# K loads of 512 KB for each batch step in place of 1 MB for two, with the order table written anew

## The chip, the cores and the metric

The kernel runs on one core of one Trainium2 chip. The metric is the device time of one execution in microseconds; the number compared is the median over runs. The profile shows one execution: its span is the time from the first to the last instruction that the profiler saw.

Names of the engines in the profile: PE is TensorE (matmuls; PEld its weight loads), DVE VectorE, ACT ScalarE, POOL GpSimd, SP the queue of SyncE, from which this kernel starts all of its DMAs. L645 is line 645 of the kernel.

## What is computed

Two independent problems A and B of the same shape, each an attention block over a given key and value cache, with their outputs side by side:

```python
B, Sq, D = 16, 80, 576
Hq, Hkv, Sk, Dh = 32, 16, 512, 128
q = (x @ wq).reshape(B, Sq, Hq, Dh).transpose(0, 2, 1, 3)
k = repeat(k_cache, 2, axis=1); v = repeat(v_cache, 2, axis=1)
p = softmax(einsum("bhqd,bhkd->bhqk", q, k) * Dh ** -0.5)
o = einsum("bhqk,bhkd->bhqd", p, v)
out = o.transpose(0, 2, 1, 3).reshape(B, Sq, Hq * Dh) @ wo      # concatenated: (16, 80, 1152)
```

All arrays are bf16. A K or V cache is 16 x 16 heads of 512 x 128, that is 128 KB a head and 32 MB a problem.

## The kernel before

**Steps.** The work is cut into 128 steps U (64 a problem). A step is one batch element and four key heads (eight query heads). Steps alternate between two groups of four heads: U = 2i and U = 2i + 1 are the same batch element with heads 4q to 4q+3 and 4q+4 to 4q+7 (line 500). Eight batch elements make a half of the batch.

**A step.** The Q projection for four batch elements and one pair of heads at a time (L565 and its tail L578 on PE, evicted to `qT` by L590 on ACT or L591 on DVE). The scores of a step are five tiles of 128 x 512: one of the remainder rows (L679, the 4 x 32 rows that don't fit in the four main tiles; one PE operation does it for two steps together) and four main tiles (L692), one for each key head. Each tile gets its row maximum on DVE (L701), the exponential with row sums on ACT (L705), a reciprocal on DVE (L711) and the scaling on POOL (L714). For two steps together the tiles are transposed on PE (L749), copied to `pT` (L766, L767, L775, L776), multiplied with V (L797), and copied to `oT` (L811, on ACT or DVE). Then comes the output projection (L843), gathered in `acc` (L855) and at the end added and stored (L872, L878).

**Loads.** All DMAs are issued by SP, in one order. K is loaded by a transposing DMA (L645) into `kT`, which holds NK = 6 steps in three pairs of slots; V by plain DMAs of 512 KB (L649) into six slots. With KSP = 0 the width `kw` (L637) is 2 for every step: the even step of a pair issues one transfer of 1 MB that writes the slots of both steps, with one semaphore, and the odd step issues none (L651). Besides these there are loads of wq (L534), its tail (L538), wo (L608) and x (L400; for problem B L461, L466, L467), and the stores.

**The order.** Every operation belongs to a stream (for example all K loads, or all exponentials). `ORDER` (L61) is a string that merges the streams into one order: each letter takes the next operation of its stream, an apostrophe ahead of it puts that operation on ACT in place of DVE where it may run on either, and digits are PSUM banks. Every engine and SP run their operations in this order. Letters that matter here: `a` K load, `m` V load, `Q` wo, `R`, `S`, `T` wq, `U`, `V`, `W` wq's tail, `X` x, `O` store; `e`, `f`, `d` Q projection for the first, the second and the later groups of heads (`h`, `i`, `g` its tails), `j` main scores, `k` remainder scores of a pair, `l` transposes, `c` product with V, `b` output projection.

The dependencies and semaphores follow from the order (`finalize`, L214). Two rules bear on loads: a load waits for the last readers of the slots that it writes (for K the scores of six steps before), and `paced` operations, that is all whose name starts with `ld`, wait for the PE operation that stands last ahead of them in the order (L240):

```python
if op.eng == "pe":
    last_pe = op
elif op.paced and last_pe is not None:
    deps[id(last_pe)] = last_pe
```

Of the kernel before, what the change touches and what calls it, by code (L numbers as in the profile page):

```python
# [66 lines left out]
cc7cc4cmmammj6d0j2wKAwd7'Bt'Btgl4315NwKCtl6G'F'Hk27F'E'Gj3j4xNwwb6j1ubtwtxj2aj3c0cNw'ytw'Atj6mc4Qcc5Qcj0d1j2tw
ANBwDCCCDCCc3mcCutd5BCtgl3674'HwNKFl0DCj5t'F'Ej1j2b3bGwNwGwtCCt'ytj5d7c0wNj6j3cwttwc4d2cs1j5CDCc6AYNwct'BCCc1'
ActCgml0436'H'K'Gl5Fk27'B'F'EGk40xj1b5wuxtxNxuuCCabc2j6mj3uwwNyd7j4cd1gwtt'Ac5j6HNwt'Ktcj0j3b2wj4wBNbc7j1twtCC
CDCDCycj5tCNwl6320'Atl4wF'Gj7c1tcmwEd3j6d5'Ft'Ggj7c2BNwNwaj0'Htj1j4cmwtc3AKNwwtDCCCCCCDCcd6c2cad7c0'BttAcCgl25  # L70
13K'B'Hl4F'Gk06'EFj2'Gj7xc4mb1j5cmbj3wuxNwt'Auj4Nwwwtt'yCCj0j2ac6cc7cj5md1tBNAwwtwNtCCDCCCDj7b6twd4c3bcttCg'yl
7520BH'Kl6G'Fk31'Ek47'F'Gxxc2mj5uxuNNwDCCCCcb6j0ubtAwxj2c1'ytwcc3j4cc5'Buj0tNwAwCDCcd1j6md2d3ttwNBd4tCggCl6057
'K'H'Kal2NHGE'G'F'Fk31j4b0Cxwuj2c6cmc7j5twxctuAwj4j3btwBNwd1j6Uj2aj7b5Ctwttc4Rj3wNwDCCt'ytcbj2d6AwtwNCDCCCc7cd
4mt'B'yd0ggl2537NKH'Hmml6j4NGEwb1CDCCCj3bj5w'F'K'GtFwtc7cj6c3j2c'y'AtNwwBtj7c4j0d5cmUc6tcj3wwNwBd1d2'AttCCCDCd
7tggl4360H'K'HKl5F'Gak17'Ek23'F'Gxc4xucc6cUj0b5j1u'AxNwBxwututCDc7cj2AwNRmbj4c0j7cj3j1b6twNwt'y'BtwNCCCCCCCDwd
2bj4d5tywttd6amd3ggl7041'K'KNHHl2'Gk63E'Fj0'F'Gxxj5uc7cuNwwAj2c4j1cc6mc'Bc3tcj4b7Ut'Bwtd5j3wNwAtd0wCCDCCCCj2tw
NDCtj6bd4wtd1tNyCggl6723'HNKK'Hl0'G'FDCCCk15'F'GEaj4j7xuxwc2cj0c6mcj3b1wAwu'Btttc6cmj5mj4bwNwAwtd7j0twNtj6d2DC
CCCCwc5d3ctd4atggyBNH'K'Hl6501CCDKNl7'Gj3Ew'Fj2j5j4c6'G'Fcc0cj1c7ct'AwBwwtj0c6c'Att'BwNb2d3j7d5j4CtCCCwNwwCtab
d6DCt'ytd7ggml2401H'K'KHl3F'Gk67'Ek24x'F'Guxc5j0cb3wxNu'Atuc6cbj7c0cmCCBxwyNuj1c6mmcj5wt'B'Atj3d2Nwwtb4j7j1d6d
5j0btwwwNCDCCDCCCttNytd7aQggl0143NK'HCCCKl2F'G'Hk76Ej0'F'Gj1xCDc5xucc4cj3j2c7Aww'Butwtwb5maj4bcj1twNwAtj0d3j6c  # L80
2Qmcd7CDCtwwNtCCtd1ByNtd4gDCCHgl6520'H'KNKFl3'Gk41'Ej5'G'Fxj7mCuxwwc2cc0cj3j6'Auttac4cb2BAwwd0j5j1j4mbc7twNtwt
tNwj3d6cCCCCDwtd1Cd5tBygKNgl2437'H'H'Gl6FNE'K'G'Fj0b1CCwj2j3twwj5Qbj6mc0twcd2c7cj4'yttwNAwCCDCt'Btd3j1c5gcj6Nw
wd0c4md7cCCDC'AttKHgl3526mmBH'Kl1F'Gk04Gk73'F'Exab1j5c2cc6xuxuwNDCCcj4j0bNBxwwu'Atuc6cj2j7c5tAwNwDCCCCtj3acb4t
'Bd6j0twNwd5mj2btd3tzwNztd0gOgl2471'H'HCCCCKKl6'Fk03Exx'Gj5j2c4'G'FcuAwNwuc7j6cj1QOc0mc'Bc3tcj7b4Aw'BttwwNj0j5
ad2btwtwNj6td3CCDDCCCwzNtd1COd7tggl6540'K'Hl3'FKHNGk12'ECCCj5'Gxj6mXj7'Fj4xc0ucwc3ucc1ctb2j5wAww'BtttAwNj3bXd1
j0j6CwtzwNwttd4c7mcd3aOtd2DCDCCBNgCgl6705KK'Hl1NHE'G'FCCd2j4j7wwj0c6cc3c'F'GBwt'Atj1c5j4cXj3c6cwNww'At'Bttb7j6
# [870 lines left out]
```

## Time and profile before

| | |
|---|---|
| median of 3 runs | 716.97 us (712.87 to 717.15) |
| the profiled execution, its own time | 715.38 us |
| its span | 712.3 us |
| PE, ACT, DVE, POOL busy | 703.7, 647.0, 614.7, 432.6 us |
| granted TensorE clock | 1.00 throughout |
| K loads: issues, median from issue to landing | 32 of A, 8.9 us; 32 of B, 8.5 us |
| V loads: issues, median from issue to landing | 64 of A, 5.2 us; 64 of B, 5.4 us |

How to read it: a row of a group has the line, engine and operation, the tile written and those read, the shapes, the count, the busy time, the mean of one in ns, and the idle time ahead of them with what ended it. A row of a tile or line has the least, median and largest duration of one in ns, and the first and last start. A row of the timeline or of the chain starts with the start and the length in us. A row of waits has the total, the count and the longest. A row of windows has the stretch, its length, the busy time of PE, PEld, DVE, ACT and POOL, the granted clock, DMA's share and GB/s. A matmul's duration includes its way through the array, so neighbours overlap; the pace of a sequence is read from a chain piece divided by its count.

### The profile page before, as it was taken

How to read it: one execution, taken by the hardware profiler on the slowest of the kernel's cores; microseconds unless marked ns; L12 is line 12 of the kernel's file. 1: busy time of each engine (PE TensorE's matmuls, PEld its weight loads, DVE VectorE, ACT ScalarE, POOL GpSimd, SP SyncE). 2: the span in 40 equal slices, each digit the busy share in tenths (PEclk: the TensorE clock that was granted, in tenths of full speed). 3: DMA queues.
4: the chain of work that ended last, by engine and by line, in shares of the span. 5: the costliest groups of instructions: out<-in, count | busy, mean ns of one | idle time of the engine just before them, and what ended most of it. 6: DMA issues, size and time to landing. Idle time of an engine off the chain costs nothing.

```text
span 712.3 us, 26078 instructions
## 1 busy us (share of the span) xinstructions
PE 703.7 (99%) x10820; PEld 511.9 (72%) x10820; DVE 614.7 (86%) x1337; ACT 647.0 (91%) x1774; POOL 432.6 (61%) x650
## 2 busy tenths in 40 slices
PE   8999999999999999999999999999999999999998
PEld 4567767777776777777767777777777777777777
DVE  2999988888898988889989889898889989899894
ACT  2999989899998999989999899999999999999893
POOL 0667666657565575556766566665755666566663
DMA  9999999998999999999979999999999968898872
GB/s 216 261 249 262 256 230 249 285 220 212 205 229 263 240 227 226 197 261 243 240 204 210 278 247 226 198 194 260 254 209 268 219 161 234 211 254 162 225 166 73
DMA packets 374165, 160.70 MB, mean 226 GB/s; under 512 B 278560, under 2 KB 370976, under 8 KB 374048
## 3 DMA queue, kind: packets, MB, share of 16 engines
q1 hardware_dynamic: 374048, 159.05, 96.5%
q8 instruction: 85, 1.39, 0.8%
q14 instruction: 32, 0.26, 0.1%
HBM read 87.65 MB, written 2.95 MB: 127 GB/s over the span
## 4 chain that ended last, share of the span: by engine, by line
PE 92%; ACT 5%; DMA 2%; DVE 1%; issue 0%
PE ps L843 21%; PE ps L797 19%; PE ps L565 18%; PE ps L692 15%; PE ps L749 10%; PE ps L679 4%; ACT p_sb L705 4%; PE ps L578 3%; DMA kT<-in_B_k_cache_dram 2%; ACT pT L766 1%; ACT qT L590 1%; PE ps L373 1%; PE ps L421 0%; ACT pT L775 0%; ACT oT L811 0%
## 5 line engine op out<-in xcount | busy, mean ns | idle before, releaser
L714 POOL TENSOR_SCALAR p_sb<-p_sb,rinv 128x512 bf16<-128x512 bf16 x640 | 430.8, 696 | 264.0 <-DVE rinv L711 263.6
L705 ACT ACTIVATE p_sb<-ps,negmax 128x512 bf16<-128x512 f32 x640 | 440.1, 720 | 14.6 <-DVE negmax L701 12.1
L701 DVE TENSOR_REDUCE negmax<-ps 128x1 f32<-128x512 f32 x640 | 411.3, 680 | 20.7 <-PE ps L692 12.9
L797 PE MATMUL ps<-pT,v_sb 128*128 128x160 bf16 x2048 | 184.7, 233 | 0.5 <-issue 0.4
L797 PEld LDWEIGHTS ps<-pT,v_sb 128*128 128x128 bf16 x2048 | 154.4, 98 | 39.1 <-ACT pT L775 2.9
L843 PE MATMUL ps<-wo_sb,oT 128*128 128x288 bf16 x1280 | 180.1, 286 | 0.3 <-ACT pT L766 0.3
L692 PE MATMUL ps<-kT,qT 128*128 128x512 bf16 x512 | 169.0, 380 | 1.7 <-ACT p_sb L705 0.9
L565 PE MATMUL ps<-xT,wq_sb 128*128 128x320 bf16 x1024 | 167.5, 299 | 0.7 <-DVE xT L429 0.5
L843 PEld LDWEIGHTS ps<-wo_sb,oT 128*128 128x128 bf16 x1280 | 122.9, 98 | 42.9 <-ACT pT L766 2.2
L705 ACT ACTIVATION_READ_ACCUMULATOR p_sb<-ps,negmax 128x1 f32 x640 | 150.5, 235 | 0.0
L565 PEld LDWEIGHTS ps<-xT,wq_sb 128*128 128x128 bf16 x1024 | 96.8, 98 | 43.5 <-ACT p_sb L705 2.0
L766 ACT COPY pT<-ps 128x512 f32<-128x512 f32 x182 | 99.6, 602 | 6.3 <-PE ps L749 4.4
L749 PEld LDWEIGHTS ps<-ident,p_sb 64*128 64x128 bf16 x5120 | 82.7, 95 | 8.0 <-issue 1.3
L591 DVE TENSOR_SCALAR qT<-ps 128x320 bf16<-128x320 f32 x125 | 56.9, 484 | 36.3 <-PE ps L578 35.9
L749 PE MATMUL ps<-ident,p_sb 64*128 64x64 bf16 x5120 | 86.0, 190 | 0.5 <-DVE qT L591 0.5
L590 ACT ACTIVATE qT<-ps 128x320 bf16<-128x320 f32 x131 | 52.7, 443 | 24.2 <-PE ps L578 23.9
L811 DVE CAST oT<-ps 128x320 bf16<-128x320 f32 x135 | 64.3, 481 | 9.0 <-PE ps L797 8.8
L692 PEld LDWEIGHTS ps<-kT,qT 128*128 128x128 bf16 x512 | 45.2, 97 | 30.6 <-ACT pT L766 5.4
L811 ACT CAST oT<-ps 128x320 bf16<-128x320 f32 x121 | 53.3, 453 | 1.9 <-PE ps L797 1.7
L767 DVE COPY pT<-ps 128x1024 bf16<-128x1024 bf16 x74 | 49.3, 685 | 4.8 <-PE ps L749 4.3
L711 DVE RECIPROCAL rinv<-rowsum 128x3 f32<-128x3 f32 (+1 forms) x256 | 40.2, 161 | 4.0 <-ACT p_sb L705 3.6
L679 PE MATMUL ps<-kT,qT 128*32 128x512 bf16 x512 | 37.0, 383 | 1.0 <-DMA kT<-in_B_k_cache_dram 1.0
(33 smaller groups left out, 151.4 us busy)
## 6 DMA issues: line engine op xcount, KB each, us to landing
v_sb<-in_A_v_cache_dram SPq DMA_DIRECT2D x64, 512.0 KB, 5.2
v_sb<-in_B_v_cache_dram SPq DMA_DIRECT2D x64, 512.0 KB, 5.4
wo_sb<-in_A_wo_dram SPq DMA_DIRECT2D x8, 576.0 KB, 5.7
wo_sb<-in_B_wo_dram SPq DMA_DIRECT2D x8, 576.0 KB, 5.0
wq_sb<-in_B_wq_dram SPq DMA_DIRECT2D x4, 1024.0 KB, 6.9
out_dram<-osb SPq DMA_DIRECT2D x40, 72.0 KB, 3.7
wq_sb<-in_A_wq_dram SPq DMA_DIRECT2D x8, 256.0 KB, 4.4
wq_sb<-in_A_wq_dram SPq DMA_DIRECT2D x2, 1024.0 KB, 6.9
```

The costliest lines, as they stand in the source:

```text
L565: last = e.matmul(ps[:, vbq[h].phys, QO:QO + 320], lhsT=wq_sb[:, wsl, ck, hi * 128:(hi + 1) * 128], rhs=xT[:, half, ck, n0:n0 + 320], star ...
L590: return e.activation(dst, src, AF.Identity, scale=SCALE)
L679: last = e.matmul(ps[32 * g4:32 * g4 + 32, vb_.phys, :], lhsT=qT[:, qsl_, bl_, g4 * 160 + 128:g4 * 160 + 160], rhs=k_of(U_, g4), start=Tru ...
L692: return e.matmul(ps[:, vb.phys, :], lhsT=qT[:, qsl, bl, gl * 160:gl * 160 + 128], rhs=k_of(U, gl), start=True, stop=True)
L701: return e.tensor_reduce(negmax[:, si:si + 1], ps[:, vb.phys, :], axis=AX.X, op=AluOpType.max, negate=True)
L705: return e.activation(p_sb[:, psl, :], ps[:, vb.phys, :], AF.Exp, bias=negmax[:, si:si + 1], scale=1.0, accum_out=rowsum[:, ss, k:k + 1])
L714: return e.tensor_scalar(p_sb[:, psl, :], p_sb[:, psl, :], rinv[:, ss, k:k + 1], 1.0, op0=AluOpType.mult, op1=AluOpType.mult)
L749: last = e.matmul(dst, lhsT=p_sb[64 * h:64 * h + 64, psl2[i_][k_], j * 128:(j + 1) * 128], rhs=ident[64 * h:64 * h + 64, 64 * h:64 * h + 6 ...
L766: return e.copy(dst.bitcast(F32), ps[:, vb.phys, :].rearrange("p (j n) -> p j n", j=4))
L797: last = e.matmul(ps[:, vo.phys, off:off + 160], lhsT=v_sb[:, vs, gl, j * 128:(j + 1) * 128], rhs=pT[:, pts, j, :, 32 * gl:32 * gl + 32], ...
L811: return (e.copy if en == "act" else e.tensor_copy)(dst, src)
L843: last = e.matmul(ps[:, vb.phys, 0:DC], lhsT=oT[:, sp_ * (HH // 2) + i, rb * 128:(rb + 1) * 128], rhs=wo_sb[:, 2 * c3 + sp_, i, :], start= ...
```

## The change

Two lines of code change, two constants and the order table. `kw` is now 1 for steps with KSA <= U // 2 < KSP, which is all of them, so each of the 128 steps issues its own transposing DMA of 512 KB into its own slot, with its own semaphore; the place of the data in `kT` is as before. The wait for a slot's last readers and the pacing now hold for each step by itself. Nothing else in the code changes.

```diff
-KSP = 0
+KSA = 0
+KSP = 64
...
-            kw = 2 if goct >= ILV and U // 2 >= KSP else 1
+            kw = 1 if KSA <= U // 2 < KSP else 2
...
-                      dsem="d_k%d" % ks, name="ldk%d" % U, stream="K")
+                      dsem="d_k%d" % ks, name="ld%s%d" % ("hk"[kw - 1], U), stream="K")
```

The functions around it, unchanged:

```python
def em_ldk(e, kc_ap=kc_ap, b=b, q=q, ks=ks, w=kw, il=goct >= ILV):
    src = kc_ap[b, 4 * q:4 * q + 4 * w, :, :].rearrange("g (p j) d -> (g p) j d", j=4)
    if il:
        dst = kT[:, ks // 2, :].rearrange("p (j n) -> p j n", j=4)[:, :, ks % 2 * 512:(ks % 2 + w) * 512]
    ...
    return e.dma_start_transpose(dst, src)
```

The order table is replaced as a whole: 5180 operations before, 5244 after, the 64 added ones all K loads. Its first three lines, before and after:

```diff
-XXSSVVTvv!PSSan2o7o3PZo5'ZZTe6o2e4r5o7!ZZYe0e3WWhIThf1'J'IJe4e6Te0he7e2r5hae3'I'I'J'YJe4e7hhf0'I'I'Jmj5j6k2wxJ
-tf4f3uiwij7'M'Ltj5wLf2f1j0X'MtNwtif4wMLj7f6tiaCCwNj5'MXf1m'LwCDCtk3j0xf6twiuLj4'Mtj2NwDCCj5e7j3e0wwNtthwk46'Jt
-Ixl1027tCC!xul5Gj3'Ff4maGNwp1'Fu'EDj7Zwf5ij1j2mc0ctLwNt'Atc6j3cj4e7wNwBte0hj6twNIw'J'MtCCCDCCCCC!aj2j1c3cc0cw'
...
+XSSVVSSXTvv!Pn3r1o4o7o5'ZYPZ'Ze2e6aTTWWTe1e3e7he5e4hI'JI'Je0hf2ho3o6'J'Z'JIIZf5aaaaXaj6wj4j1j0mk7f3wtwtmf6f4tw
+xuf1i'Mtiie7NLLNL'Me2f5!CDCf0'Mj1iwr3'Mj4'LYk0f6j5wtxtwuj3Xamhf1j4Iw'Jte0j7wwtj2e5tmhaij3twINk70me4NMwCCCCDCCx
+t'J'Lte1hj3j6uxINwNwl7425'Juj1'Gf0Fwtf4til7Ltk63FxNCCDCCCCj0ae7j1'G'Ewutc2cwj6f5At'Me0f2p4wNxCCDtihaj1c6u'L'IZ
...
```

More of the change, by code (lines that the diff above doesn't have):

```diff
@@ L67 @@
[L67 to L86, printed above, removed]
@@ new lines @@
+ZtCcxc6cC'Axl0247uBl1uFj6'Fj3Ej0'Gj5md1w'Gs4d2c7wtYwtcamj6c4twNwAcj3gd0Ct'BtwNHj5d7j4c6'KtwwNk12gcamc3CCCDCCt'
+H'KNxxad5cj0d7wgmaDCCutu'BHKNACd1j4td5wgl7623'KtHl0j1j4b5aGwF'F'G'Ej3j0Nwwtd2mj7j1c6bctwtNwwtCCCCDCtac3d0cNAyj
+7CCDgc5cj6'B'Htwc3ck14KwAt'Btxj0l3257l6xuGuj1d2Nwb4'E'F'Fj3'GNwwc6cj5tDCCCCd7tAwtmQgj6Qc0cj1KNwwj3mabCDttHNwtc
+5CCmacj6c1ACc'Bt'ywk57Btl3402xl1G'Fd6'E'Fud4j3j1xGwb0j5uwwNNtd2j7wtc3ctANc1cgk53CCCK'B'Htj1xxuj4bc6wcc7j5utyNw
+ws0j3c'Ytb1j0wDCCCDCCtbt'BAwNyaml3654CCDl1FGtj7j3d0'E'GwNwagj5'HtwFc4cj2d6md7'Ktt'Awj0gc3cwNKNc1CCDCCCCcamj5ac
@@ new lines @@
+4Aw'H'Btttcj7d2d3j0BwgtwKl5146'Hl7Gk32'F'EtxFj5d1xu'Gb4j7j0uwwNbc2j6tDCCtwyNwCtcj5c3k47matwNxNxCDCCab0cbt'AuuN
+yj5c6cc0mj7j2wBcd3'Atw'BCCDtamgwl0546'H'Kl7GNtj1b3FwCCCC'F'G'Ej2wj7d5k64twtj1txxNwuubc0cj7j2ytc6caAwNwc4cj3d0c
+1'BtctCCDCb7awABNtgUl1246'K'HCCCl3'G'F'Fk50Nxbj2'Eu'Gywxd3mmc7j4cj1twb5j2w'Auttwd6j7c0acd4wBNtc1j0bCCDCtwNyd2t
+CDCCggH'H'Kj5cc7wcUt'Aml4360BNl7mGj5j1'F'G'K'Ej4b3wwttwNFbc2j0cj7w'ytNw'Atc3j6cj2c5cj4RmaatCCDCDCCCd1c7j0wwBNw
+wtd6mmcd3'AtCtBCd5tggl0274H'K'HKl1F'Gk56'Ek23xc7'F'Gxucc0cj4xwBNxuut'Aub1c6cj5CCDbj2j4wAwt'ytc7j6j3j5NwwNtCCCD
@@ new lines @@
+CwNwb0d1ctt'BCd4d6aj2btNwytd3CDCggal7205'K'KNHHl1'G'FCCk43Ej6xj2'F'Gc7xuj1cc0j5cAwuc4cRj7'BUc3Umawtcb0twANww'B
+td4j6j2mmbj1d3DCCCtwtwNwtCtd7CyNd6tggl5102KNK'H'HCCCl3'Gk46E'Fj1xj7c0c'F'Gxuc3cj5j2b4u'BwAwtac3acj6twAwNwbj1tt
+Cwtd7j3Nwd0j2tCCDDCd5amc6cmtCwyBNtd1CDggCl3246NH'K'Hl0'Gj7aKE'Fj1j2'Gj5CCwc3'Fcwc6tcBw'Ac4cc7j0cmj3tw'At'Btj6b
+1wNwNwDCCCCbj2d7td4aw'yttd1td0ggl3256H'K'KHl4F'Gk07Ek31'F'Gxc4aj5b6cxuwuxNc0cmmDCCxBt'Auuc2bj0mcj4j7c1Nwwy'Atc
+aj5d2j3b6twBwNCCCDCttj4j1d7d0bNwwwtCCtyNtd3DCgNKgl1645m'H'HKCCl7F'Gk32Ej1'G'Fj6xc5cxuAuc7cj0j4wc3'Bwtwtwttb5j7
@@ new lines @@
+abcj6wANwCtj0md2td3j7c4caNwwtd6CDCCCtd1myBggl7540HNN'K'HDCCCl2FK'Gk36'Ej5xj7c1'F'Gcj2uwx'Ac0mQj4cc3cwBAwb1uttt
+j6j0baj3d7aQwNwtwtwc4j2d5cd6attwNyCDCCCtd0CgNBKNgl2413'H'Kl7mCCCDCFj0b5'F'G'G'HEwj1twj4c7j2bj3cwtNwd0t'ytwCtj4
+j6d1wAwNCDCCj5c2gcc3ctt'B'Ac4wHcmad6d0gKBl3241t'KHl7'F'E'F'Gk56Gamk30xxuj4b1c2cuwNxxc5'AutuCCcj6bj7Qc3BwNwtcc5
+cj2j0j4mCCDAwt'BtwNwztj3b6twNCCCDCbj7d0OtwztQOd2d1d6ggl7435NKNK'H'Hl2aDCCCCk61E'F'Gj7xj0c3'G'Fxucc4j2caj5c6uww
+Ac'Bc1tcwwAb4j7'Btj3tNwtwCCDtj1d6mbj0Xtd2wzNwtd5CtCd4ggXl0137'K'HKNHDCl4'FGNk62'ECCmOj0'Gxj1j5'Fmj3xc7ucwc4ucA
@@ new lines @@
+wc6cwAwc7b2t'Btj4j0ttj6j1bawNwtCCDCtNwCd5cd3d4wBzttd6gamOgl1702NHNHKCCC'Kl6E'G'Fj5'F'Gj4d3wc1j0camc2wt'AtcwBc7
+cj6j5c1j2'Atcamd4b7Nwwwt'Bgj1j6tCCDCtNwwCCDCbd2d0gzKtt'K'Hl6415Hl7'Gak30E'Fk42x'F'Gxuxuc6b1j5cbxNuDCCuc7cj0c2O
+j3cNwzwwt'A'Bc5Ct'AtcOaj4j6BCj7Nwwtwtb1j2aj0bd5NwttCDCCd6CgXl3724wNzHtOml0'Kmak61'G'F'E'GFxxNCDCb7j2uwd5j3j6c4
+cj0wuwtt'Atbd2j1NwzwCCCj4c3cd6td7aOj0wNwtc1gmg'BtCCCDj3md4c'K'HNHKwAtd2c6acj7twgl5310'B'HCl4tKGEk26R'G'F'Fj3mb
+7xwNxCCuj0c5q4bj1ctuw$zNc2acj6c7wBwt'#'Atcd3c5j0ANwtCCCcj4md1d2twDCDtNBd7CgCgl4506K'K'H'FHl1Gj2'Fj7Ead4Oc3cj1j
@@ new lines @@
+5b0wwGt'AtwNwtj6c3cCDCCc7wctmc2j1UNAcwj5j7t'BbCNwwzttt'Bd3d1CCd0CDggl2756UUm'K'H'Kl3HG'Fk40G'EOk27'Fxc6cxuamj3
+j5c1cxwNwxu'A'Btb4tuCCc6j0bacj5Rj3b1wNwtu'Aj2c0cj7d6wNwtDCCCCtzBwtj5Ud4NwtCDj3d0btwCzNtd2CCggl3157NHKF'K'Hl6'G
+k40'EGj3'Fxxj1Oac5cuAwwd7amc2cc6u'BtcmXc0j4Xcj2Aj6d5twgj1b3wN'Bttj0wwNHwCCCCDDCC'Kttj2wbd4j1d5twztgl2607'H'Kl3
+tk45GNFxxN'Fmd1j3CCDCC'E'Gj2c6cj0c7OcXuwud4'BAwtc5aOd7j6cwtNwd3tAgtgHNj0c5DCCC'Kc'KwHj2'Bd1wCtl5346aatFGNl7DCj
+0'F'E'Gd2wgj3c4'Htcc5j6cj7KwwNBwCCtt'Ac0cc2Nq1mmj5j6d3c'Atj4d0DCCCwwBb7j2tbwN$wt'#tCtCgzKl4615Ol7'HF'Gk20x'G'E
@@ new lines @@
+xumj6j3k45muFxb2aubc7xNwutCCcj4c1ad5j0cj6wzwAtNwCDt'Btad3c4j2wwNtgcj7j1d0tHNwwCCDCC'AttCc6cOab5d2NK'BgCl4137K'
+Hl6'Fj2'Fj0wd4d6'E'GtGwgQk13c7bNxxHztCCD'Kucj6Oj2wwmc4d5j1u'Atmj7acc0cj6d3atwNwBtCDCCj2tj1c4wwwN'AttCcb7BNbCDC
+gtl0462'HzNKl1'Fk37'EGxCCCj4'F'Gwj0mc5ucc6j2cj1wtb3wxwtj4tbutwNzCDCtc2camj0j7d3BwAwtj1c6twNcd5d4td0CABOaggHNCC
+l1267'K'FKGHl3j0j5'F'ENwwtCDCb2j1mOatj3bc0j6cc4wwGNzwtt'Acj5c1'BtCDCcj0c4j7cd3wwNwt'Bd2t'AtmQmamd4CCCd5ggml701
+6K'K'G'HHl2Fk45'F'EGk70xj6wuj3b2bc4j1xtuxwzNwxNCCcj5ut'Atuc2mj6cb7awBwtQj1c4cac0j3cbwNtCCCtd5j6NwAwNd4'B'yttd2
@@ new lines @@
+DDCCCCd1aggl6703K'H'KHNl4CC'G'Fmk51Ej2'F'Gxmj7c0wuj6cc4wcj3'Atc5tBxwwutb0cj4wANj2d7tj1bc6j5wtCDCCDwytcd3twNd0N
+Btd1CgCCCgl5426NKF'H'Kl7ak31'G'H'F'GEj5j4xxj0c2cc6cj7uwwub3awtt'Bj1bj4j5c6AwtwNwDCCDCCttcd0mmj2c7catwANwd1Ctd6
+Ctd4yBggl7235H'K'KHNl0'Gj6Ew'FCCj1j2'G'Fj4c3cwc7tcAwNt'BQc0cd6j5j3twNwAb1c2ttacj4j0'Bwd5tNwwtCCCDCDCCbmd3ytd4g
+gal2701H'K'HKl5G'Fk46'Ek73'F'Gxj2b0xuxuxubj1mc6cac5cmj4uwNywwNc3t'A'BtCcc0j2acj7wNBj5ttwNwj1d6CCCwt'Atb0j2d4bt
+Nwd3'ytd1DCCCCDggl0572DC'K'KHHNGl6'FOk13CCC'Ej4'F'Gxj5c7cmxuAwwuc0cj6b2ammj7j1c3w'BttcwbtAwNtj3c4j0wtwNcd5tj1d
@@ new lines @@
+7tCCCDCwmd3d0tNyBggKl1246'Hl7KHG'FCCk05'Ej3m'F'GNxxCCDc1acc2cj4c7cwu'ABuj0wj1j6tj2wb5twANwaabttj7d3wDCCc0j4d1c
+'yttwwNNBtad5Cd2tCggNHl6074'K'Hl1R'Gj5j3CCCCDKFwj6w'G'Et'Fwtj2b0c7cj5c4cc1cj3AwwNttNwc7cbj6tt'A'BBd5j2mwwyCCCD
+CUd7Uttd3d4ggl2016K'H'K'GHl5Fk34'EFOk20'Gxc5acaj7xuj1c6cb3xBxNwwCCu'Auutj6bmb4j0Nwttj2j7bj6Uc5wNytcwwAwyNtc0d3
+j5d2d1ctCCCDDCCwNBtDCCCd7tmggal4560KNK'H'Hl2R'GCk71E'Fj3'G'Fxj5Umamc6cxuwuc0j2cj4c7ct'BwAwb1wtj3td0j6d5tNwwj2b
+tAwtCDCCj4c3wNcmCtd7d2tCgagBNyNKl4136'H'KHGl5'Fk70'Ej4'Gj1c3cc6DC'FxxAuCCj5j2amacuwb3w'Btwtwtc6j0cd7wNAj1ttbj4
@@ new lines @@
+wNwtDCCCCmj5d6c2d0cwNyBtCd1tCDCggl4325'HKKN'Hl7'Gj6Ew'Fj1j3j0Cc2'G'Fcmwc4tcwBtc5d7cc4aj6ANwwc'At'Btj2ab5mtj3ww
+Nj1bd0CCtCCCDtwyd4d3tggl1526'H'K'KHl7G'Fk03m'EGk41'Fxc6cxuxc5j7cc2ac'AuNBAwxNmc0cj6u'Btub2j3j0bwwtCCCb5j6twtj3
+QNywwd4j1d7aj0d2btCCCDNwwtCDtt'yd6g'Hgl0531'KCl4KHE'G'Fk27j6xNj5'G'Fuxwwj0c3j1cc4cuQmmb2abj7tt'BNwAwtwNj3c5cc0
+j6j4twtd1ctd7wNAwtd5CCDCCDCCCCd3tBNyggl4062'H'HKNKl1maam'Gk37E'Fj0CDCxj5c6'F'Gcxuj1c4cj2wuwAb3twc7tj6wtwNbcj0c
+5j1t'AtBwCCCCd2j4wNwtd7cd6tCDtByNd1Cgaal4350gH'Kl2j7'G'F'E'HKj1b3Fwwj2wttbj4j7c5cc1GNNwwt'y'Atj0cc6cj3wt'BtAwN
@@ new lines @@
+CDCDCCCCd5j4c2d6d1ctwBtd0CCggl2734H'K'KGHl5a'Fk06'Ek72'Gxc1'Fxcj4uAc5macj3j0uj1mb6wwwN'BttNxCbmj5b4CCwwt'ytutc
+3j6bxwNCCDCtucj7aj0d5NzwNAwttDCCd6c1d2cd4'BCCDggl1703'H'KKHGl5mmaO'Fk62'Ej7'G'Fxj1xNwc4cj0j5c3cub6AwBwutttj2Nw
+wtDCCCj4d7c3j1cmbj5c0cwtwztOaQd2twNCCd6td4CABNggl5301NHHG'K'Kl2'Fk64'Ej7xCCDCj5c0'F'GwCucj2j3c1cwxAwb6t'Btad7j
+0j5c1cbwwNAutDCCtc1j3twzwNtcj4d6CCwBNtQd5d2tCCggKNKl4130'HHCDl7Cj2E'G'Fd5j1'F'Gwc3caj6c0j7cwtwAt'Bwtc4cj2mmmc1
+acd0j6Nw'Attd4j7BNwwDCCCCtb3j1tbwtd7zggl3162KH'K'Hl0G'Fk47'Ek51G'FxOmOc2xucac3cj0c6cwNxx'A'BuCc2d4cb3utuAj5j6N
@@ L128 @@
+tmj5c6cc7j2bwtCCDtwNAc'BCj0z'Bk65wtCl7134xtOl2xb0E'F'F'GGj7j3c2wj1uuNwbj4ctc5j6twNzwCCDCCtcc0cc1j3ct'ABNwAj4wN
+'Bttj5k20b7mxxwubmODCCCCwl2631utl0tNzFCj7'F'Gj4j2EwNww'GtOb5tbc6j0cc1ctNw'B'Ac2ctc3mDCCCCCDcb7'BANzCbCl1642l0G
+zb3'EG'FFbc4cc2OcOc0cAz'BAOc4cb5Bbb4zbOzO
 """
```

49 lines of the change are left out of this document (6 added, 43 removed).

## The prediction

> **What bounds the kernel now.** I read the page first: busy shares, then the chain that ended last, then the DMA queues.
>
> ```profile
> span 712.3 us, 26078 instructions
> PE 703.7 (99%) x10820; PEld 511.9 (72%) x10820; DVE 614.7 (86%) x1337; ACT 647.0 (91%) x1774; POOL 432.6 (61%) x650
> q1 hardware_dynamic: 374048, 159.05, 96.5%
> HBM read 87.65 MB, written 2.95 MB: 127 GB/s over the span
> PE 92%; ACT 5%; DMA 2%; DVE 1%; issue 0%
> ```
>
> TensorE is busy 99% of the span and is 92% of the chain. The change removes none of its matmuls, so little can be won: TensorE's free time is 712.3 − 703.7 = 8.6 us. On the other side stands DMA, whose packets take 96.5%. But that share counts packets in flight, not a full wire, as the rate in 0.5 us slices shows (first line from 230 us on, second from 400 us on).
>
> ```profile
> GB/s 68 367 381 158 43 125 252 363 375 385 373 299 148 22 145 290 290 306 259 11 144 290 282 290 288 291 290 289 291 257 25 178 371 381 231 112 136 334 357 335
> GB/s 292 289 290 120 169 247 325 326 378 390 375 387 381 328 354 348 350 346 347 320 193 44 19 228 289 291 290 289 291 291 88 80 295 383 327 168 177 290 289 290
> ```
>
> Plain loads (V, wo) reach 380 GB/s, K transposes 290, and each change between the two leaves a dip: on the way in 299, 148, 22, 145 (614 where four slices at 290 are 1160, so 0.95 us lost), on the way out 257, 25, 178 (about 0.8 us lost). A run of K transfers between other DMAs so costs about 1.75 us of turnover. Next, who waits for K.
>
> ```profile
> PE ps L679 <- DMA kT<-in_B_k_cache_dram: 1.0, 1, 1.0
> PE ps L692 <- DMA kT<-in_A_k_cache_dram: 0.8, 1, 0.8
> 404.19 9.08 SPq L645 DMA_TRANSPOSE kT<-in_B_k_cache_dram  x1
> 404.19 12.71 DMA kT<-in_B_k_cache_dram
> 417.03 0.71 PE ps L679 x8
> ```
>
> TensorE waits for K twice, 1.8 us in all. The last three lines are the worse of the two: the transfer issued at 404.19 stands behind 6 us of plain loads (the second line of slices runs at 320 to 390 until 410), is served after that, and its products start at 417.03.
>
> **The change part by part.** Base: the profiled execution, span 712.3 us, time 715.38 us; the median of the runs, 716.97, lies 1.59 above it.
>
> Evictions. The two order tables give nearly the same split: of the 256 copies to oT, 141 instead of 135 on DVE, of the 40 to the accumulator 29 instead of 23. All streams together, with the durations below and their like, ACT has 2.3 us less to do and DVE 2.2 more, against 65 us that ACT and 98 us that DVE are idle in the span. Priced at nothing; if that idle time were not there, it would be 2.2 us.
>
> ```profile
> L811 DVE CAST oT<-ps 128x320 bf16<-128x320 f32 x135 | 64.3, 481 | 9.0 <-PE ps L797 8.8
> L811 ACT CAST oT<-ps 128x320 bf16<-128x320 f32 x121 | 53.3, 453 | 1.9 <-PE ps L797 1.7
> L855 DVE COPY acc<-ps 128x288 f32<-128x288 f32 x23 | 10.3, 446 | 1.3 <-PE ps L843 1.0
> ```
>
> SP's queue. 64 issues of 1 MB become 128 of 512 KB, among the same 128 of V and 96 others.
>
> ```profile
> L645 SPq DMA_TRANSPOSE kT<-in_A_k_cache_dram x32: 3927/5944/9075, 6.0 to 323.2; - x32
> L645 SPq DMA_TRANSPOSE kT<-in_B_k_cache_dram x32: 3975/5514/9544, 344.0 to 674.2; - x32
> L461 SPq DMA_TRANSPOSE xT<-in_B_x_dram x2: 3458/4235/5012, 256.3 to 333.5; - x2
> L649 SPq DMA_DIRECT2D v_sb<-in_A_v_cache_dram x64: 367/507/3432, 22.5 to 355.7; - x64
> ```
>
> K holds SP 32 × 5.94 + 32 × 5.51 = 367 us, V some 128 × 0.5 = 64, the 96 others at V's pace some 50: SP is free over 200 us. What an issue costs beyond its bytes the trace does not show. Lowest: nothing, or some tens of us less than nothing, if a short transfer stands less long against a full queue. Highest: the line through the least 1 MB row (3.93 us) and the least x row (3.46 us for 640 × 512 × 2 bytes = 0.655 MB; 1 MB is 1.049 of those) leaves 2.7 us at no bytes, 64 × 2.7 = 173 us in all, which nearly fills SP. I take 0.37 us, the least that a V issue holds SP, the nearest row for an issue with little behind it: 24 us, hidden in SP's free time.
>
> DMA. HBM's 90.6 MB hold all but the transposed loads, so those are 159.05 − 90.6 = 68 MB: 236 us at 290 GB/s, and the rest 238 us at 380. In the old table K stands in 61 runs with other DMAs between, in the new one in 89 (59 of one half, 23 of two, 5 of three, 2 of four). Before: 474 + 61 × 1.75 = 581 us. After: 474 + 89 × 1.75 = 630 us of 712. The added cost is nothing at the lowest (turnovers overlap with what drains) and 67 × 1.75 = 117 us at the highest (each half turns over alone); I take 49 us, as the dips above stand between kinds: inside one kind only the dip 259, 11, 144 is seen. It lies in DMA's free 130 us; on the path it is nothing as long as the loads are issued early enough, which is the next point.
>
> One page speaks against the change, and for the first rival below. The Trainium skill, DMA: Bandwidth & Descriptors, section Bandwidth, tells to gather transfers to 1 MiB or more; its table (0.95 us for 64 KB, 6.15 us for 1 MB) gives, as an estimate by a line, 0.6 us for each additional transfer and 38 us for 64. The 512 KB V loads in the slices, back to back near 380 GB/s, don't show this loss; by that estimate too the sum stays inside DMA's free time.
>
> Earliness. A K load waits for the PE op that stands ahead of it in the table, and what is queued on SP behind it (V, wo, stores) waits with it. I add up PE's work in the table from that op to the first product that reads the load, at the paces of the chain:
>
> ```profile
> 399.67 2.17 PE ps L565 x16
> 70.37 1.96 PE ps L843 x16
> 75.50 1.11 PE ps L797 x16
> 68.20 0.24 PE ps L578 x2
> 69.62 0.75 PE ps L692 x3
> 68.45 1.17 PE ps L749 x80
> 78.02 1.09 PE ps L679 x16
> v_sb<-in_A_v_cache_dram SPq DMA_DIRECT2D x64, 512.0 KB, 5.2
> kT<-in_A_k_cache_dram SPq DMA_TRANSPOSE x32, 8.9
> xT<-in_B_x_dram SPq DMA_TRANSPOSE x2, 6.3
> ```
>
> Old table: least 10.6 us, median 15.2, for a load that lands in 8.9. New table: the first half of a pair has a median of 20.7 us, the second 15.2, and 4 of the 126 after the first pair have under 10 (least 8.6). Half a transfer lands between 5.2 (plain, same bytes) and 8.9 us; I take 6, next to the x row. The transfer of the 417 us wait had 10.6; its halves have 17.7 and 14.6. V's earliness is the same in both tables (median 17). So I take back 1 of the 1.8 us that TensorE waits for K, with bounds of −1.8 and, if the least early halves each meet a queue like the one at 404, +4 × 1.0.
>
> The added wait on PE. The product of the remainder heads (L679) covers two batch steps and now waits for two semaphores. Lowest nothing; highest, if each costs a stop like the issue stops of L578, 64 × 0.27 = 17 us. I take nothing: the loads landed long before.
>
> ```profile
> PEld ps L578 <- issue: 18.3, 69, 0.3
> 6.04 6.42 SPq L645 DMA_TRANSPOSE kT<-in_A_k_cache_dram  x1
> 16.44 0.59 PE L692 MATMUL ps<-kT,qT 128*128 128x512 bf16 x2
> 9.00:17.00 8.00, 7.88 (x61) 4.36 (x60) 1.52 (x4) 3.22 (x9) 0.00 (x0) 1.00 0.99 200
> 0.00:100.00 100.00, 97.44 (x1388) 64.31 (x1389) 83.73 (x184) 85.96 (x240) 55.75 (x90) 1.00 1.10 245
> ```
>
> The start. The first scores run at 16.44 us; ACT, the fourth busy number, works 3.22 of the 8 us ahead. In the new table four groups of four Q products and two of their tails fewer stand before the first scores: 4 × 0.54 + 2 × 0.24 = 2.7 us earlier. Against it, the first K load moves behind two Q groups, from 6.04 to about 7.5 us, at half the bytes. Bounds −2.7 and +1.5; I take −1.
>
> Sum: −1 − 1 = −2 us, span 710.3, time 713.4; on the median 716.97 − 2 = 715.0 us. A difference of 1% (7 us) is about what a measurement of this kernel can tell from no change, and mine is below it.
>
> **The rivals.**
>
> A full DMA queue: every half pays its own turnover, also next to another half. Place: the first 100 us, at 245 GB/s, 24.5 MB. Old: 12 K transfers 43 us, the rest 31, 12 × 1.75 = 21, sum 96 of 100. New by the table: 22 halves 40 us, the rest 29 (two V fewer), and 22 × 1.75 = 38, sum 107; with turnovers by run, 16 × 1.75 = 28, it is 96 again. It decides from 1.44 us a half on. The later stretches of 100 us would have 98 to 106 in the same way, so the loss is 7 us at least and some 20 if nothing is made up: 724 to 736, say 728. For it: the dip within one kind, and SP's 9.08 us when it stands behind loads. Against it: that dip is one, while other 1 MB stretches run flat at 290.
>
> More bubbles by the new order: ACT's 5% of the chain (35 us) grows by a quarter, 9 us: 726. Against it: the median PE work between a pair's transposes and its first V product is 1.1 us in both tables, and between its last scores and its last transposes 6.7 in the old and 7.1 in the new.
>
> Faster: the start's whole 2.7 us, K's whole 1.8 and a tenth of ACT's share, 3.5: −8 us, 709. Against it: that would take nearly all of TensorE's 8.6 free us.
>
> The change doesn't free the first half earlier: in 11 of 64 pairs the table has both halves within 1 us. This would lose my 1 us for K at most, and is part of the forecast.
>
> **How the numbers follow.** Forecast (711 to 721 by itself): 0.60. Full queue: 0.22. Bubbles: 0.10. Faster: 0.08. The first gives the time, 715.0. The range 708 to 730 leaves out about half of the faster case and a third of the full queue's, with a little of the bubbles: 0.15. Faster by over 1%: 0.07, most of its case; slower by over 1%: the full queue, the bubbles and a little of the forecast's rim, 0.32; within 1%: 0.61.
>
> **What would show it.** Right: K's SP row near 2 to 3.3 us a half; no more than about 90 turnovers, with two adjacent halves flat at 290 GB/s; waits of TensorE on K under 2 us; first scores by 16 us; a PE share of 99%. Wrong: an SP row whose halves stay above 3.9 us, K or V among TensorE's releasers with several us, a dip behind every half, or a larger ACT share of the chain.

## The result and the profile after

The changed kernel takes 720.63 us (median of 20 runs, 716.88 to 725.07) against 716.62 us for the kernel before (20 runs, 712.87 to 720.63). The ratio is 1.0057 with a 95% interval of 1.0042 to 1.0072, that is some 4 us slower: within the 1%, but the other way than the forecast of -2 us. The profiled execution took 717.32 us with a span of 715.6 us, at a granted clock of 1.00.

The page after, the lines that answer to those of before (the code stands two lines lower, L645 is now L647):

```profile
span 715.6 us, 26172 instructions
PE 706.5 (99%) x10820; PEld 511.8 (72%) x10820; DVE 616.1 (86%) x1342; ACT 646.6 (90%) x1769; POOL 431.9 (60%) x650
q1 hardware_dynamic: 376096, 159.05, 103.1%
PE 96%; DMA 2%; DVE 1%; ACT 0%; issue 0%
```

TensorE is still the bound. ACT's share of the chain fell from 5% to 0. In the DMA queue, the same bytes took 103.1% of 715.6 us in place of 96.5% of 712.3: 737.8 less 687.4, 50 us more packet time.

Four views of the changed kernel, a fence for each: the rows of the K loads on SP, TensorE's waits for K and wo (total, times, longest), the first scores in the timeline, and the window of the first 100 us.

```profile
L647 SPq DMA_TRANSPOSE kT<-in_A_k_cache_dram x64: 1644/3812/8096, 8.3 to 336.0; - x64
L647 SPq DMA_TRANSPOSE kT<-in_B_k_cache_dram x64: 1720/3154/6567, 340.5 to 679.6; - x64
```
```profile
PE ps L681 <- DMA kT<-in_A_k_cache_dram: 0.5, 1, 0.5
PE ps L845 <- DMA wo_sb<-in_A_wo_dram: 1.5, 1, 1.5
```
```profile
14.45 1.04 PE L694 MATMUL ps<-kT,qT 128*128 128x512 bf16 x4
```
```profile
0.00:100.00 100.00, 96.08 (x1280) 61.47 (x1281) 81.67 (x179) 82.38 (x229) 52.88 (x86) 1.00 1.09 232
```

By the medians, K now holds SP 64 × 3.81 + 64 × 3.15 = 446 us. Summed over all issues it is 468 us against 367 before: 102 us for 64 more issues, 1.6 us each. The waits for K shrank from 1.8 to 0.5 us and the first scores run 2 us earlier.

The forecast had two halves that follow each other run as one flat stretch. They don't. The rate in slices of 0.5 us from 95 us on:

```profile
GB/s 51 307 387 371 178 2 10 186 290 289 191 74 152 291 289 192 25 270 340 345 229 284 318 205 7 9 119 285 344 327 290 290 290 148 18 266 389 369 251 287
```

The halves issued at 93.95 and 98.47 us run at 290 from 99 and from 101.5 us, and between them stand 191, 74, 152, some 0.8 us lost. At the 39 places where a half follows a half the second lands a median of 2.2 us after the first; 512 KB at 290 GB/s would take 1.8.

In the first 100 us TensorE is busy 96.08 us where it was 97.44, at 232 GB/s in place of 245. I subtracted from the time, at each point, the TensorE work started by then at full pace. What is left is idle time; before and after it is 2.3 and 3.7 us at 25 us, 4.6 and 5.8 at 55, 5.7 and 9.6 at 100, 7.3 and 11.0 at 200, 12.6 and 15.9 at 700. The whole difference of the two executions has arisen by 100 us: 1.2 us of it by 55 us, the rest between 55 and 100.

One of the places in it, the wait for wo (timeline, then two pieces of the chain: this load of wo, and the half of K behind the wait of 0.5 us):

```profile
92.16 1.15 PE L845 MATMUL ps<-wo_sb,oT 128*128 128x288 bf16 x8 [1.47 <-DMA wo_sb<-in_A_wo_dram]
```
```profile
83.97 8.14 DMA wo_sb<-in_A_wo_dram
101.97 7.08 DMA kT<-in_A_k_cache_dram
```

A load of wo that is issued at 83.97 lands after 8.14 us. The page gives a median of 6.6 us for A's wo loads after and 5.7 before, where TensorE waited for none.

### The profile page after: what moved, and what is told of

It is laid out like the page before. It is cut to its first block, busy times and chain, and to the rows that moved or that the text cites. A ratio compares the mean times of both kernels' runs of the same rounds, so it can differ in the third digit from the quotient of the medians.

```text
span 715.6 us, 26172 instructions
## 1 busy us (share of the span) xinstructions
PE 706.5 (99%) x10820; PEld 511.8 (72%) x10820; DVE 616.1 (86%) x1342; ACT 646.6 (90%) x1769; POOL 431.9 (60%) x650
## 3 DMA queue, kind: packets, MB, share of 16 engines
q1 hardware_dynamic: 376096, 159.05, 103.1%
## 4 chain that ended last, share of the span: by engine, by line
PE 96%; DMA 2%; DVE 1%; ACT 0%; issue 0%
PE ps L845 22%; PE ps L799 20%; PE ps L567 19%; PE ps L694 16%; PE ps L751 11%; PE ps L681 4%; PE ps L580 3%; DMA wo_sb<-in_A_wo_dram 1%; DVE negmax L703 1%; DMA kT<-in_A_k_cache_dram 1%; PE ps L375 1%; PE ps L423 0%; DVE qT L593 0%; ACT p_sb L707 0%; PE ps L443 0%
## 5 line engine op out<-in xcount | busy, mean ns | idle before, releaser
L707 ACT ACTIVATION_READ_ACCUMULATOR p_sb<-ps,negmax 128x1 f32 x640 | 147.9, 231 | 0.0
L813 DVE CAST oT<-ps 128x320 bf16<-128x320 f32 x141 | 66.9, 478 | 4.5 <-PE ps L799 3.8
L813 ACT CAST oT<-ps 128x320 bf16<-128x320 f32 x115 | 49.9, 446 | 4.8 <-PE ps L799 4.7
```

The lines of the kernel that those rows point to most:

```text
L707: return e.activation(p_sb[:, psl, :], ps[:, vb.phys, :], AF.Exp, bias=negmax[:, si:si + 1], scale=1.0, accum_out=rowsum[:, ss, k:k + 1])
L813: return (e.copy if en == "act" else e.tensor_copy)(dst, src)
```

## The experiments

All times are ratios to the kernel before on the same chip (its median there: 715.62, 717.1, 715.54, 715.29 or 715.75 us), with a 95% interval. "Old" and "new" are the two order tables. 1% is 7.2 us.

**Theories after the result.** (1) The halves: each costs SP and DMA time that isn't hidden. (2) The new order of the other operations costs. Rivals: the cost is TensorE's own (two semaphores at one product), or the one wait for wo is all of it.

**E1 and E4: the split alone, in the old order.** In E1 each `a` becomes `aa`, both halves at the old place; in E4 the second half stands some operations later, so that there are 111 runs of K between other loads.

```diff
-            kw = 2 if goct >= ILV and U // 2 >= KSP else 1
+            kw = 1 if U // 2 < KSP else 2
-XXSSVVTvv!PSSan2o7o3PZo5'ZZTe6o2e4r5o7!ZZYe0e3WWhIThf1'J'IJe4e6Te0he7e2r5hae3
+XXSSVVTvv!PSSaan2o7o3PZo5'ZZTe6o2e4r5o7!ZZYe0e3WWhIThf1'J'IJe4e6Te0he7e2r5haae3
```

> The old order table with each 1 MB K transfer written as two adjacent ones of 512 KB (61 runs of K, as before). Theory A, the split itself fills SP's queue and DMA in the first 125 us: slower than before by 2 to 5 us, SP late there by more than in the old kernel, a load other than V among TensorE's releasers. Theory B, the new order alone costs (its start and the place of two wo loads): within 1 us of before.

> The old order table with halves, the second half of 61 pairs moved behind the next DMA in SP's order: 111 runs of K in place of 61. If a turnover costs about 1.75 us and lies on the path in the first 125 us (theory A), slower than the adjacent halves by 3 us or more; if the added cost lies in the issue of a half whatever stands beside it, the same as the adjacent halves within 1 us; by theory B within 1 us of before.

Measured: E1 1.0105 (1.0068 to 1.0141), E4 1.0382 (1.0346 to 1.0419). The split by itself costs 7.5 us, and much more with the second halves late: in E4 TensorE waited 11.1 and 5.4 us for K in two groups. E4 so mixes lateness with the number of runs, and I draw only the first from it.

E1's waits for K are longer than its rows of waits say (1.0 us). At 84.03 us the remainder product L680, which reads both halves of a pair, starts after 1.91 us of idle time that the profile puts down to ACT. But the last ACT result that this product needs was ready by 82.2 us, while the second half, issued at 77.90 us, landed at 83.79. Counted by landing, four such products (at 84, 250, 368 and 425 us) waited 5.3 us for a second half.

**E2 and E5: the new order without the split, and with it but not earlier.** E2 sets `KSP = 0` and keeps each pair's `a` at the place of its second half; E5 issues both halves there.

> The new order table with 1 MB K transfers: the first half's letter of each pair is taken out, the transfer stands at the second half's place (for the first pair at the first half's). Theory A: the queue empties, within 1.5 us of before. Theory B: slower than before by 3 to 5 us, as the changed kernel is.

> The new order table, both halves of a pair issued together at the second half's place (the first pair's as in the changed kernel). It differs from the new order with 1 MB transfers only in the splitting, and from the changed kernel only in where the first halves stand. Theory A (a half costs SP and DMA more wherever it stands): slower than the new order with 1 MB transfers, which was 6 us over before, by 2 to 8 us. Theory B (the split is free, the order costs): the same as it within 1.5 us. If the early first halves are what the new order was written for, the changed kernel beats both.

Measured: E2 1.0081 (1.0052 to 1.011), E5 1.0182 (1.0149 to 1.0216). The split costs 1.0% in the new order too (E5 over E2). From E5 to the changed kernel, that is by the earlier place of the first halves, 1.25% or 9 us come back. The new order with 1 MB transfers loses 5.8 us, which I had priced at nothing.

What E2 lost in its profiled execution isn't a wait for K. TensorE stopped four times, 6.4 us in all, where it had no semaphore to wait for; the longest as a piece of the chain:

```profile
52.76 2.87 issue
```

Ahead of the end of each of these stops, by 2.4 to 2.6 us, one 16 KB packet of the instruction queue (q8) starts. That TensorE stood still for its own instructions is read from this and was not tried.

**E3: wo earlier.** The changed kernel with the loads of wo that TensorE waited for four DMAs ahead.

```diff
-H'KNxxad5cj0d7wgmaDCCutu'BHKNACd1j4td5wgl7623'KtHl0j1j4b5aGw
+H'KNxxad5cj0d7wgmaDCCutu'BHKNACd1j4td5wgl7623'KtHl0j1j4b5QQaGw
```

> The changed kernel with the two wo loads for which TensorE waited at 92 us issued four DMAs earlier in SP's order, ahead of two K halves and two V loads. Theory A and B both: that wait of 1.5 us goes, 1 to 1.5 us faster than the changed kernel. If SP is simply full there (A), K or V behind them is late in its place and at most 0.5 us is won.

Measured: 1.0047 (1.0023 to 1.0071), not told apart from the change; a gain of 1 to 1.5 us would not stand out from this interval either. The wait for wo is gone from the waits of TensorE; in its place stands another (timeline of E3):

```profile
154.41 0.46 PE L799 MATMUL ps<-pT,v_sb 128*128 128x160 bf16 x4 [2.53 <-ACT p_sb L707]
```

So the one wait is not all of the cause: without it the kernel is still over the one before.

**E6 and E7: where the split costs, in the old order.** E6 splits pairs 12 to 63, E7 pairs 0 to 11, both halves at the old place.

```diff
+            kw = 1 if U // 2 >= KSP else 2     # E6, KSP = 12
+            kw = 1 if U // 2 < KSP else 2      # E7, KSP = 12
```

> The old order table, 1 MB transfers for the first 12 pairs of steps (about the first 130 us), two adjacent halves from then on. If the split costs only where SP is full, in the first 130 us: within 1.5 us of before. If it costs everywhere: 3 to 6 us over before, the later part of the 8 us that halves throughout cost.

> The complement: the old order table with adjacent halves for the first 12 pairs and 1 MB transfers after. If the split costs only where SP is full: 5 to 8 us over before. If it costs everywhere alike: 12 of 64 pairs, under 2 us.

Measured: E6 1.0072 (1.0043 to 1.0101), E7 1.0080 (1.0053 to 1.0107). 12 pairs at the start cost as much as 52 later ones. But in neither profile is the cost spread over the pairs: the larger part of it is one late second half and the slower clock behind it (last section), in E6 at 364 us with a wait of 4.06 us, in E7 at 85 us with a wait of 2.83 us. By the times at which the same operations of TensorE end, E6 falls 6.6 us behind the kernel before at its place, and E7 4.4 us at its own.

**E8: the old first loads.** The changed kernel with the second load of x back at the front, and a transpose of x with its copy (`r`, `Y`) behind the first Q products.

```diff
-XSSVVSSXTvv!Pn3r1o4o7o5'ZYPZ'Ze2e6aTTWWTe1e3e7he5e4h
+XXSSVVSSTvv!Pn3o4o7o5'ZPZ'Ze2e6r1YaTTWWTe1e3e7he5e4h
```

> The changed kernel with the old kernel's start: the second x load back ahead of the wq loads, and the transpose of x's tail and its copy behind the first two Q products. If the new start costs what TensorE's idle time up to 12 us shows (0.7 to 0.9 us more than in the old kernel) and nothing gives it back: 0.5 to 1 us faster than the changed kernel, which was 4 us over before. If the loads late around 90 us set the pace, no gain.

Measured: 1.0045 (1.0026 to 1.0063). This edit wins nothing that can be told from the change.

**E9 to E12: less to load.** From the seventh on, a V load brings two of its four heads (the products of the others read what lay there; 32 MB less). E9 is the kernel before with this, E10 is E1, E11 is E5, E12 the changed kernel.

```diff
-                return e.dma_start(v_sb[:, vs, :, :], src)
+                return e.dma_start(v_sb[:, vs, 0:n, :], src[:, 0:n, :])
```

> The kernel before, with two of the four heads left out of every V load from the seventh on (the products read what an earlier step left there): 32 MB less to move, the same instructions. It is the base of the next three. Theory C (loads that come late because SP and DMA are nearly full; the split takes capacity) expects up to 3 us less than before, the loads that were late. If loads play no part, the same.

> The old order with two adjacent halves for each K transfer, V loads cut in the same way. Theory C: the 7.5 us by which halves were slower shrink to under 2 us against the kernel before with the same cut. Rival D (a half costs on TensorE itself, by its second semaphore wait, or by instructions, whatever DMA does): still 6 us or more over it.

> The new order with both halves together at the second half's place, V loads cut in the same way. It was 13 us over before, 9 over the changed kernel. Theory C: within 3 us of the kernel before with the same cut. Rival D, or a fault of the new order that has nothing to do with loads: 5 us or more over it.

> The changed kernel, V loads cut in the same way. Theory C: its 4 us go, within 1.5 us of the kernel before with the same cut, perhaps under it. Rival D or the order by itself: still 3 to 5 us over it.

Measured, all to the kernel before: E9 0.9931 (0.9911 to 0.9951), E10 0.9933 (0.991 to 0.9956), E11 0.9996 (0.9971 to 1.002), E12 0.9984 (0.9963 to 1.0005). The DMA rows of E9 and E10:

```profile
q1 hardware_dynamic: 342816, 127.06, 80.5%
```
```profile
q1 hardware_dynamic: 344864, 127.07, 87.2%
```

With the queue at 87%, the split costs nothing that can be told in the old order (E10 as E9, within some 2 us), and the place of the first halves is worth nothing (E11 as E12 within the intervals). The cost of the split is therefore one of late loads in a nearly full queue, as E1's landings say too, and not one of TensorE: the two semaphores are still there in E10. But the new order keeps a loss of 0.5% (E12 over E9), 3.8 us with an interval of some ±2, which this relief doesn't take away. The relief begins with the seventh V load, 50 to 57 us into the kernel, so it couldn't help in the first 50 us.

**E13 to E18: exchanged starts.** E13, E15 and E17 begin with the old table and 1 MB transfers and go on, from the operation given, with whatever is not yet done in the order of the new table and in halves. E14, E16 and E18 begin with the new table in halves and go on with the old one in 1 MB. PSUM banks after the seam are renamed so that they fit.

```diff
-KSA = 0
+KSA = 11          # E13; 19 in E15, 7 in E17
-KSP = 64
+KSP = 11          # E14; 19 in E16, 7 in E18
```

> The old kernel up to the loads of step 22 (its first 705 operations, about 91 us of TensorE's work, K in 1 MB), then the new table with K in halves to the end. Theory 'start': the 4 us lie in what the new table does in the first 90 us, so this run stands within 1.5 us of the kernel before (ratio 0.998 to 1.002). Theory 'throughout': they are spread over the new table, so this run loses what the rest of the span holds, about 3.5 us or more (1.005).

> The counterpart: the changed kernel up to the loads of step 22 (its first 719 operations, about 91 us of TensorE's work, K in halves), then the old table with 1 MB transfers. Theory 'start': 3 to 5 us over the kernel before (1.004 to 1.007). Theory 'throughout': within 1.5 us of it.

> As e13, but the old kernel to 178 us of TensorE's work (1342 operations, steps to 38), then the new table in halves. Theory 'start': within 1.5 us of the kernel before. Theory 'throughout': about 3 us over it (1.004).

> As e14, but the changed kernel to 178 us of TensorE's work (1361 operations, steps to 38), then the old table with 1 MB transfers. Theory 'start': 3 to 5 us over the kernel before, as in e14. Theory 'throughout': about 1 us over it (1.0015).

> The old kernel up to the loads of step 14 only (its first 418 operations, 55 us of TensorE's work), then the new table in halves. At this cut both tables have done exactly the same operations. The run with the old start to 91 us had no loss against the kernel before. If the loss lies in the first 55 us, the same here: ratio 0.998 to 1.001. If it lies between 55 and 91 us: about 4 us over (1.004 to 1.007). If in both: between.

> The counterpart: the changed kernel up to the loads of step 14 (its first 426 operations, 55 us of TensorE's work), then the old table with 1 MB transfers. If the loss lies in the first 55 us: 3 to 5 us over the kernel before (1.004 to 1.007). If it lies between 55 and 91 us: within 1 us of it.

Measured:

| seam, TensorE's work | old start, then new | new start, then old |
|---|---|---|
| 55 us | E17 0.9993 (0.9977 to 1.0009) | E18 1.011 (1.0086 to 1.0134) |
| 91 us | E13 0.9994 (0.998 to 1.0009) | E14 1.0053 (1.0027 to 1.0079) |
| 178 us | E15 0.9978 (0.9966 to 0.999) | E16 1.0066 (1.0048 to 1.0083) |

Theory "start" holds in five of the six; E18 lost more than either theory had said. E17 puts the start into the first 55 us of the table: with them taken from the old kernel the loss is gone. With an old start the rest of the change costs nothing, and E15 is 1.6 us faster than the kernel before, the fastest of the kernels that compute the whole. With a new start the loss is there whatever follows. E18 loses more than the change itself. Its waits of TensorE from 50 to 80 us, and its windows:

```profile
PE ps L680 <- DMA kT<-in_A_k_cache_dram: 3.6, 1, 3.6
```
```profile
60.00:65.00 5.00, 1.44 (x82) 1.20 (x78) 1.80 (x3) 2.95 (x7) 1.88 (x3) 1.00 1.07 252
65.00:70.00 5.00, 4.42 (x24) 2.21 (x25) 2.35 (x5) 2.12 (x6) 1.36 (x2) 0.66 1.10 250
```

The last half ahead of the seam is issued at 58.10 us and lands at 65.54, and the old order reads it at once. This is the seam's doing: where both have done the same TensorE work, E18 is 0.6 us behind the kernel before at 58 us and 6.7 us at 67. So E18 by itself doesn't show what the start costs; E14 and E16 do. E14 is 2.9 us behind at the seam, and another 3.1 us come where the kernel before stands at 100 us, most of them by these waits:

```profile
PE ps L750 <- ACT p_sb L706: 1.2, 1, 1.2
PE ps L798 <- ACT p_sb L706: 1.1, 1, 1.1
```

The second of them is a wait for V: the ACT result that the product needs was ready at 103.33 us, the V load landed at 104.75, and the product started at 104.88.

**What the start does.** SP's timeline of the changed kernel, start and length, where the new table stands:

```profile
14.51 10.55 SPq L647 DMA_TRANSPOSE kT<-in_A_k_cache_dram  x4
...
38.01 4.48 SPq L647 DMA_TRANSPOSE kT<-in_A_k_cache_dram  x1
42.54 0.59 SPq L651 DMA_DIRECT2D v_sb<-in_A_v_cache_dram  x1
43.17 7.54 SPq L647 DMA_TRANSPOSE kT<-in_A_k_cache_dram  x2
...
56.23 4.74 SPq L647 DMA_TRANSPOSE kT<-in_A_k_cache_dram  x1
61.02 0.59 SPq L651 DMA_DIRECT2D v_sb<-in_A_v_cache_dram  x1
61.65 4.55 SPq L647 DMA_TRANSPOSE kT<-in_A_k_cache_dram  x1
```

and of E17, with the old start:

```profile
39.36 5.63 SPq L647 DMA_TRANSPOSE kT<-in_A_k_cache_dram  x1
45.43 1.69 SPq L651 DMA_DIRECT2D v_sb<-in_A_v_cache_dram  x2
47.16 6.41 SPq L647 DMA_TRANSPOSE kT<-in_A_k_cache_dram  x1
53.62 1.68 SPq L610 DMA_DIRECT2D wo_sb<-in_A_wo_dram  x2
57.63 0.92 SPq L651 DMA_DIRECT2D v_sb<-in_A_v_cache_dram  x2
58.60 6.50 SPq L647 DMA_TRANSPOSE kT<-in_A_k_cache_dram  x1
```

In these rows a half that stands alone between V loads holds SP 4.5 to 4.7 us, a whole megabyte 5.6 to 6.5. By 66.2 us the changed kernel has issued K for 12 steps, by 65.1 us E17 for 14, and both eight V loads. From 14.5 to 125 us SP is never free in the changed kernel; in E17 it is free several times, the longest from 55.30 to 57.63. Measured from the TensorE operation ahead of a K or V load in the table to its issue, the median delay from 25 to 125 us is some 4 us before and in E17, and almost 10 after.

Late loads aren't all of it. In E12, where this delay is some 4 us, and in E2, where it is some 3, the new start still loses. There TensorE stops near 52 us with no semaphore to wait for, 1.01 us in E12 and the 2.87 us of E2, again with an instruction packet ahead. Such a stop doesn't stand in the changed kernel's profile in its first 100 us.

That the start loses in general can be read at points where two orders have done the same TensorE work. Against the kernel before, the profiles of the ten kernels with the new start are 0.2 to 1.4 us behind at 26 us, and 0.6 to 2.5 at 58 us (E2 4.6); the nine that still have it at 91 us are 2.3 to 4.7 behind there (E2 6.7). The four with the old start, 1 MB transfers in it and whole V loads (E6, E13, E15, E17) are between 0.4 us ahead and 0.2 behind at 60 us.

What has arisen by 25 us is small. A row of the timeline and one of the windows of the kernel before, then the same two of the changed kernel:

```profile
6.16 0.72 PE L565 MATMUL ps<-xT,wq_sb 128*128 128x320 bf16 x4 [0.52 <-DVE xT L429]
```
```profile
14.00:25.00 11.00, 11.00 (x79) 5.53 (x78) 8.24 (x17) 9.30 (x28) 3.06 (x5) 1.00 0.98 188
```
```profile
7.03 2.89 PE L567 MATMUL ps<-xT,wq_sb 128*128 128x320 bf16 x20 [0.46 <-ACT xT L430]
```
```profile
14.00:25.00 11.00, 10.90 (x76) 5.22 (x75) 8.44 (x18) 8.32 (x25) 3.37 (x5) 1.00 1.10 194
```

The Q products begin 0.9 us later here, but that is mostly a difference of executions: in E3, whose first operations are the changed kernel's, they begin at 6.23 us. ACT, the fourth busy time of the windows, does 1 us less from 14 to 25 us (8.67 us in E3, 0.6 less). What these put off is argued from the rows and was not tried by itself, except for the first loads (E8), which won nothing.

## Why the prediction was wrong

The failed step is **the start**. I took -1 us, with bounds of -2.7 and +1.5, from how much earlier the first scores would run. They do run 2 us earlier. The price of the start is the change less E17: 1.0057 - 0.9993, that is 0.64% or 4.6 us, with an interval of some ±1.6 us. It holds the order of the first 55 us and the split of their seven pairs together. I had priced the head of the table by its first product alone, and not by what the loads and engines have ready 55 us later.

Step by step:

- **The bound.** Right: TensorE 99%, 96% of the chain.
- **Evictions at nothing.** Right for the split between the engines (DVE 1.4 us more, ACT 0.4 less). The order as a whole, which I priced at nothing beside the start, does cost nothing from 55 us on (E13, E15, E17).
- **SP's queue, 24 us.** Mis-sized: 102 us, 1.6 us an added issue in place of 0.37, inside my upper bound of 173. "Hidden in SP's free time" is right from 55 us on and wrong with the halves at the old place: there the split alone costs 7.5 us (E1), and none that can be told when the queue has room (E10).
- **DMA, 49 us.** The queue's packet time rose by 50 us, but that share counts packets in flight, so this isn't a measurement of the turnover. A turnover inside one kind, which I put at nothing, is there: with 0.4 us at each of 39 places it would be some 16 us more, an estimate. That it is nothing on the path "as long as the loads are issued early enough" is what the runs show in both directions: 7.2 us lost in E5 over E2, 9 us won back by the earlier first halves.
- **Earliness, -1.** Right in sign and in the waits for K (1.8 to 0.5 us). Its worth was too small: the earlier place pays for the whole cost of the split. The two nearly cancel, and what remains, E15's -1.6 us (-2.4 to -0.7), happens to be near my -1.
- **Two semaphores on TensorE at nothing.** Right within some 2 us: E10 has them and loses nothing that can be told against E9.
- **The rivals.** "Full DMA queue" named the right place, the first 100 us, and its mechanism is seen there (a dip also between adjacent halves, SP without a free moment, delays of almost 10 us); its price of 12 us was too high, and after 100 us it doesn't go on as I had put it. "Bubbles by the new order" came near in sign and size (9 us put, 4.6 found), but not in its place: ACT's share of the chain didn't grow. Neither was shown to be the whole cause. "Faster" did not happen.
- **What would show it.** K's SP row is 3.8 and 3.2 us a half where I wanted 2 to 3.3 for right and over 3.9 for wrong, so for A it stands between the two. Two adjacent halves flat at 290 GB/s did not come; the dip behind a half, a mark of wrong, did. The waits for K, the first scores and TensorE's share said right. None of these marks looked at the first 100 us as a whole, where the answer was.

What stays open: which part of the new table's first 55 us does it. The four halves in a row at 14.5 us, the single ones between V loads, and the changed order of the Q products were not tried apart. The split alone in the old start costs as much (E7), but by one late half and its half clock more than by anything spread out. The new start without a split costs as much too (E2), but by stops with nothing to wait for. Neither is what the changed kernel's profile shows: there seven loads landed less than 0.7 us ahead of their first product from 82 to 110 us, where the trace of the kernel before shows three.

## What to carry to other kernels

Price the first stretch of a statically ordered kernel by itself, by how far loads and engines have come at its end, not by the first product. Where a wait has several conditions, ask of each when it was met: the profile names only the last signal, and here it put waits for K and V down to ACT. Splitting a transfer in a nearly full queue costs time unless the first part is also issued earlier; weigh the two together. And when two orders differ everywhere, exchange their starts at a point where both have done the same work: it finds the place of a loss that no row of waits shows.
